# Attention feeding a soft mixture of experts: batch softmax steps moved ahead of V products, token maxima read from copied logits, exp(-m) added by TensorE

## The chip, the core and the metric

The kernel runs on one core of a Trainium2 chip. The core has a matrix engine (TensorE, PE in the profile; its weight loads are listed apart as PEld), a vector engine (VectorE, DVE), a scalar engine (ScalarE, ACT), a general engine (GpSimd, POOL) and SyncE (SP), which here only issues transfers. Every engine works through a queue of its own in order and waits on semaphores for the others. Matmuls write to PSUM, which this kernel uses as eight banks of 512 fp32 values per partition; everything else lies in SBUF. The metric is the time of one execution on the device in microseconds.

## The reference

Two parts follow each other. Attention over 8 batches, 12 heads, 448 positions and 64 columns has one unusual term, exp(-m), in the denominator; a soft mixture of experts then mixes all 3584 tokens into 32 slots and back.

```python
scores = scale * np.matmul(q, k.transpose(0, 1, 3, 2))
m = np.max(scores, axis=-1, keepdims=True)
e = np.exp(scores - m)
attn = e / (np.sum(e, axis=-1, keepdims=True) + np.exp(-m) + 1e-09)
x = attn @ v                                  # 3584 tokens x 768
logits = x @ phi                              # 3584 x 32
d = softmax of logits over the tokens         # each with + 1e-09 in its sum
slot_out = relu(d.T @ x @ w1) @ w2            # 32 slots, 4 for each of 8 experts
c = softmax of logits over the slots
return c @ slot_out                           # 3584 x 768
```

## The kernel before

**Pairs and slots.** The 96 heads are taken in 48 pairs n = 0 to 47 (NPAIR is 48), two heads in the two halves of the partitions; six pairs make a batch b. After a ramp written out by hand, the loop over s (line 758) runs one pair per turn in two half slots, y = 0 and 1. The order of the calls in that loop is the order of each engine's queue; a planner is not used. A half slot hs = 2s + y calls, in this order:

- `As` and `Bk`: score matmuls in one direction (`A`, lines 274 to 307) whose row maxima VectorE takes straight from PSUM (`mx`), and in the other direction (`Bk`, lines 352 to 404), with the maxima subtracted by a second matmul and the exponential taken by ScalarE (lines 372 and 402).
- in y = 1 the transposes of q and k of a later pair (`T`, line 256, copied out at line 263 by ScalarE or at 265 by VectorE), and for every third pair `W2` and `W3`, which turn the maxima and compute exp(-m) into the small tile `ec` (lines 345 and 348).
- `AV` (line 436): the exponentials times V. V has a 65th column of ones (D is 64), so the denominator falls out as one column of each of the seven blocks of `ps_av`. Of the 32 products of a pair, 12 come in y = 1, 12 in the next y = 0, and then 8 more for the last 64 positions.
- the functions in `post[hs]`, the batch softmax steps described below (line 788).
- in y = 1 `PX` (lines 494 to 507), which turns a finished pair of tokens into `xT`; in y = 0 the last 8 `AV` products and `N1` (line 449), a ScalarE copy of `ps_av` into `ubuf`; in y = 1 `N2` for that pair: VectorE adds 1e-9 and `ec` to the denominators (line 464) and takes the reciprocal (line 465), then GpSimd multiplies (lines 469, 479 and 480).
- transfers, copies of V and weight loads, all issued or done by GpSimd.

**Batch softmaxes.** `P(b)` returns six steps that run while the next pairs are in work, at half slots 2(6b + 8) + 0, 1, 2, 4, 5 and 9 for most batches. Step 0 multiplies x by phi (`l_mm`, 24 small matmuls, line 535), copies the logits from PSUM into `l`, a part of the tile `lb` (`l_ev`, ScalarE, line 558), and takes each token's maximum over the slots from PSUM (`c_max`, VectorE, line 562). Step 1 transposes the copied logits (`l_turn`, line 570), takes a column maximum (line 572) and subtracts the token maxima (`c_sub`, GpSimd, line 577). Step 2 spreads the column maximum (line 582), forms the running one (lines 583 and 585) and subtracts it (line 591). Step 3 takes exponentials (lines 596 and 601) and rescales the sums (line 607). Step 4 transposes one of the softmaxes (line 627, copied out at 628) and step 5 adds 28 small matmuls (line 623) to the sums (line 632).

**PSUM.** Score tiles `ps_a` and all PSUM tiles of the batch steps share one ring of three banks (`psA`); `ps_b`, `ps_t`, `ps_m` and `ps_x` share one of four (`psB`); `ps_av` has one bank. A new tile of a ring waits until the one three (or four) places earlier has been read.

Of the kernel before, what the change touches and what calls it, by code (L numbers as in the profile page):

```python
# [10 lines left out]
AX = mybir.AxisListType  # L11
AF = mybir.ActivationFunctionType
ALU = mybir.AluOpType
# [13 lines left out]
W65 = 65  # L27
# [4 lines left out]
def kernel(  # L32
# [10 lines left out]
    nc = tc.nc  # L43
    B, H, S, D = q.shape
# [112 lines left out]
    with ExitStack() as at:  # L157
# [182 lines left out]
        def W3(g):  # L340
            t = psm.tile([128, S], BF16, tag="mT", name="mT")
            nc.scalar.copy(t, st["ps_m"][:, 0:S])
            mT[g] = t
            e = psm.tile([128, NP, 7], F32, tag="ec", name="ec", bufs=3)
            nc.scalar.activation(e[:, :, 0:6].rearrange("p l (i h) -> p i l h", i=3),
                                 ngm[g][:, 0:18].rearrange("p (i l h) -> p i l h", i=3, h=2),
                                 AF.Exp, scale=scale)
            nc.scalar.activation(e[:, :, 6], ngm[g][:, 18:21], AF.Exp, scale=scale)
            ec[g] = e


# [69 lines left out]
        def AV(n, i, qs):  # L421
            g, pl = divmod(n, NP)
            if i == 0 and qs[0] == 0:
                av[n] = av_tile(n)
            a = av[n]
            if n == NPAIR - 1 and i == 0 and qs[0] == 3:
                av_half["ps"] = psA.tile([128, 512], F32, tag="a", name="ps_av")
            for u in qs:
                for hl in range(2):
                    if u < 3:  # L430
                        c0 = (2 * u + hl) * W65
                        o, qc = a[:, c0:c0 + W65], slice(u * 128, (u + 1) * 128)
                    else:
                        t, z = (av_half["ps"], 0) if n == NPAIR - 1 else (a, 6 * W65)
                        o, qc = t[64 - 64 * hl:128 - 64 * hl, z:z + W65], slice(384, 448)
                    nc.tensor.matmul(o, eT[n, i, hl][:, qc], vp[g % 2][:, 2 * pl + hl, i, 0:W65],  # L436
                                     start=(i == 0 and u == 0 and hl == 0) or (u == 3 and i == 0 and n == NPAIR - 1),
                                     stop=(i == 3), skip_group_check=True)

        av_half = {}  # L440
        on_pool = lambda n: n < NPAIR - 4
# [10 lines left out]
        def N2(n):  # L452
            g, pl = divmod(n, NP)
            b, pb = divmod(n, PB)
            u = us[n]
            eng = nc.gpsimd if on_pool(n) else nc.vector
            rec = psm.tile([128, 7], F32, tag="rec", name="rec", bufs=3)
            e = ec[mg(n)][:, group[n][1], :]
            if n == NPAIR - 1:
                nc.vector.scalar_tensor_tensor(rec[:, 6:7], av_half["ps"][:, D:W65], 1e-9, e[:, 6:7],  # L460
                                               op0=ALU.add, op1=ALU.add)
                nc.vector.scalar_tensor_tensor(rec[:, 0:6], u[:, 0:6, D], 1e-9, e[:, 0:6], op0=ALU.add, op1=ALU.add)
            else:
                nc.vector.scalar_tensor_tensor(rec, u[:, :, D], 1e-9, e, op0=ALU.add, op1=ALU.add)
            nc.vector.reciprocal(rec, rec)
            x = xb[b % 2]
            c = pb * 128
            rec2 = psm.tile([128, 2], F32, tag="rec2", name="rec2", bufs=3)
            eng.tensor_mul(  # L469
                x[:, 0:3, c:c + 128].rearrange("p i (h d) -> p i h d", h=2),  # L470
                u[:, 0:6, 0:D].rearrange("p (i h) d -> p i h d", h=2),
                rec[:, 0:6].rearrange("p (i h) -> p i h", h=2).unsqueeze(3).to_broadcast([128, 3, 2, D]))
            if n == NPAIR - 1:

                for h in range(2):
                    r = slice(64 - 64 * h, 128 - 64 * h)
                    nc.scalar.mul(x[r, 3, c + 64 * h:c + 64 * h + 64], av_half["ps"][r, 0:D], rec[r, 6:7])
                return
            eng.tensor_scalar(rec2, halfm, rec[:, 6:7], None, op0=ALU.mult)
            eng.tensor_mul(  # L480
                x[:, 3, c:c + 128].rearrange("p (h d) -> p h d", h=2),
                u[:, 6, 0:D].unsqueeze(1).to_broadcast([128, 2, D]),
                rec2.unsqueeze(2).to_broadcast([128, 2, D]))
# [32 lines left out]
        def P(b):  # L516
# [42 lines left out]

            def c_max():  # L560
                m = psm.tile([128, 4], F32, tag="cm", name="cm")
                nc.vector.reduce_max(m, v["ps_l"] if b < B - 1 else l[:, 0:4, :], axis=AX.X)
                v["cm"] = m

            def l_turn():
                if b == B - 1:
                    ps = v["ps_lT"]
                else:
                    ps = pa([128, 128], F32, "ps_lT")
                    nc.tensor.transpose(ps, flat(l[:, 0:4, :]), identf)  # L570
                m = psm.tile([128, 1], BF16, tag="sm", name="sm")
                nc.vector.reduce_max(m, ps, axis=AX.X)
                v["sm"] = m
                v["z"] = psm.tile([128, 9, NS], F32, tag="z", name="z", bufs=1)
# [75 lines left out]

            both = lambda *fs: (lambda: [f() for f in fs])
            if b < B - 1:
                return [both(lambda: l_mm(range(KC)), l_ev, c_max), both(l_turn, c_sub), both(s_max, d_sub),
                        both(exps, corr)] + ([c_turn, both(s_mm, s_add)] if late(b) else [both(s_mm, s_add), c_turn])
            return [lambda: l_mm([0]), lambda: l_mm([1]), lambda: l_mm([2]), lambda: l_mm([3]), lambda: l_mm([4]),
                    both(lambda: l_mm([PB - 1]), l_ev,
# [28 lines left out]
        def As(c):  # L685
            for _ in range(min(c, len(runs))):
                A(*runs.pop(0))
# [70 lines left out]
        for s in range(3, NPAIR + 1):  # L758
            for y in range(2):
                hs = 2 * s + y  # L760
                mix = len(runs) > 1 and runs[0][1] == 1 - y
                if mix:
                    Bk(s, 2 * y, mix=True)
                    Bk(s, 2 * y + 1, y, mix=True)
                else:
                    As(1)
                if mix:
                    pass
                elif s < NPAIR:
                    Bk(s, 2 * y)  # L770
                    side = int(y == 1 and len(runs) > 0 and runs[0][1] == 3)
                    Bk(s, 2 * y + 1, side)
                    As(1 - side)
                else:
                    As(1)
                if y == 0:
                    for i in (2, 3):
                        AV(s - 1, i, range(3))
                else:
                    if s < NPAIR - 6:  # L780
                        T(s + 6)
                    if s and s + 1 in firsts:
                        W2(mg(s + 1))
                        W3(mg(s + 1))
                    if s < NPAIR:
                        for i in (0, 1):
                            AV(s, i, range(3))
                for f in post.get(hs, ()):
                    f()
                if y and 0 <= s - 2 < NPAIR - 2:  # L790
                    PX(s - 2)
                if y == 0:
                    if 0 <= s - 1:
                        for i in range(4):
                            AV(s - 1, i, [3])
                        if s == NPAIR:
                            PX(s - 2)
                        N1(s - 1)
                        if not on_pool(s - 1):
                            N2(s - 1)  # L800
                else:
                    if 0 <= s - 1 and on_pool(s - 1):
                        N2(s - 1)
                if y == 0 and s and s + 1 in firsts:
                    W1(mg(s + 1))
                if y == 0 and wait_loads:
                    f, z = wait_loads.pop()
                    f(z)
                if y == 0 and s % 3 == 2 and (s + 1) // 3 < NG:
                    if s == NPAIR - 4:  # L810
                        V(NG - 1)
                    if s - 1 in half_at:
                        load_half(half_at[s - 1], 0, w_tile(half_at[s - 1]))
                if y == 0 and s - 1 in stage_at:
                    stage_rows(*stage_at[s - 1][0])
                if y == 0 and s - 2 in half_at:
                    load_half(half_at[s - 2], 1)
                if y == 0 and s - 2 in stage_at:
                    stage_rows(*stage_at[s - 2][1])
                if y == 0 and hs in rows_at:  # L820
                    load_rows(rows, rows_at[hs])
                    rows = rows_at[hs]
# [209 lines left out]
```

## Time and profile before

Three runs took 297.56, 299.5 and 299.66 us, with a median of 299.5. The profiled execution has a span of 299.0 us from its first to its last instruction.

| What | Value |
|---|---|
| span of the profiled execution | 299.0 us |
| GpSimd busy | 195.9 us, 66% of the span |
| granted TensorE clock | full up to about 254 us, 0.5 to 0.7 in the last stretch |
| main stretch of the batches | about 60 to 240 us, one batch of six pairs in 29.8 us |
| score maxima on VectorE (line 287) | 250 of 613 ns each |
| exponentials on ScalarE (line 372) | 250 of 574 ns each |
| exp(-m) on ScalarE (lines 345, 348) | 17 of 228 ns and 17 of 199 ns |

How to read it: each engine's busy time counts from an instruction's start to its end, so two neighbours that overlap in the pipeline count once. An entry of the waits names the instruction whose engine sat idle, and what ended the idle time. On TensorE the distance between the starts of two matmuls says more than their durations, which include the way through the array.

### The profile page before, as it was taken

Reading aid. Unit: us, or ns where it says so; the run is one execution under the profiler, and the core shown is the slowest. Engines: PE = TensorE matmul, PEld = TensorE weight load, DVE = VectorE, ACT = ScalarE, POOL = GpSimd, SP = SyncE. Lnnn points to the kernel's source line nnn. Section 1 sums busy time; section 2 is a strip of 40 time slices with the busy share of each in tenths; the row PEclk is TensorE's granted clock in tenths of the full one; section 3 lists DMA queues with packets and bytes.
Section 4 is the critical chain, followed back from the end, with each engine's and each line's share of the span. In section 5 each row is a group of like instructions: output and inputs, shape, how many; then the busy total and the mean of one; then the engine's idle time right before and its main releaser. Section 6 shows DMA issues by size and latency. Waiting matters only on the chain.

```text
span 299.0 us, 12398 instructions
## 1 busy us (share of the span) xinstructions
PE 271.4 (91%) x5174; PEld 162.5 (54%) x5174; DVE 249.7 (84%) x581; ACT 249.8 (84%) x559; POOL 195.9 (66%) x391
## 2 busy tenths in 40 slices
PE   5999899999999999999899999999999999996820
PEld 4445456566666566566556666656665555652100
DVE  5899799999999989999889999998999675537930
ACT  3569999999899989998989899989999987337820
POOL 8792887979696979887879697978686633000000
PEclk9999999999999999999999999999999999997555
DMA  7999998999999999999999999999799989908997
GB/s 132 147 143 208 149 138 138 188 165 188 185 204 179 184 176 202 163 182 182 202 159 184 176 199 152 196 183 196 125 150 187 213 185 263 344 10 318 380 453 322
DMA packets 47015, 58.67 MB, mean 196 GB/s; under 512 B 2800, under 2 KB 39920, under 8 KB 46704
## 3 DMA queue, kind: packets, MB, share of 16 engines
q0 software_dynamic: 40304, 42.29, 89.6%
q1 hardware_dynamic: 6656, 15.60, 13.8%
q8 instruction: 40, 0.66, 0.8%
q14 instruction: 15, 0.12, 0.1%
HBM read 89.16 MB, written 15.14 MB: 349 GB/s over the span
## 4 chain that ended last, share of the span: by engine, by line
PE 68%; ACT 10%; DVE 6%; POOL 6%; issue 4%; DMA 2%; DVEq 0%; POOLq 0%; ACTq 0%
PE ps_av L436 15%; PE ps_a L285 10%; PE ps_b L367 7%; PE ps_b L370 7%; PE ps_t L256 5%; PE ps_b L396 5%; PE ps_x L501 3%; PE ps_b L399 3%; ACT W L402 2%; PE ps_o L925 2%; DVE mx L298 2%; PE ps_s L623 2%; PE ps_h L862 2%; PE ps_so L882 2%; ACT W L263 2%
## 5 line engine op out<-in xcount | busy, mean ns | idle before, releaser
L287 DVE TENSOR_REDUCE mx<-ps_a 128x1 f32<-128x448 f32 x250 | 137.3, 613 | 4.6 <-PE ps_a L285 3.5
L372 ACT ACTIVATE W<-ps_b 128x448 bf16<-128x448 f32 x250 | 120.4, 574 | 0.0
L285 PE MATMUL ps_a<-W 64*128 64x448 bf16 x250 | 80.9, 352 | 0.0
L367 PE MATMUL ps_b<-W 64*128 64x448 bf16 x250 | 70.5, 352 | 1.1
L436 PE MATMUL ps_av<-W 128*128 128x65 bf16 (+1 forms) x1536 | 64.9, 196 | 2.2 <-issue 1.6
L436 PEld LDWEIGHTS <-W 128*128 128x128 bf16 (+1 forms) x1536 | 50.5, 100 | 30.2 <-issue 26.4
L370 PE MATMUL ps_b<-mT,sel 64*128 64x448 bf16 x250 | 66.5, 350 | 0.0
L469 POOL TENSOR_TENSOR W<-ubuf,rec 128x384 bf16<-128x384 f32 x44 | 36.3, 824 | 35.7 <-ACT W L507 19.3
L402 ACT ACTIVATE W<-ps_b 128x448 bf16<-128x448 f32 x86 | 46.1, 574 | 2.0 <-PE ps_b L399 2.0
L256 PEld LDWEIGHTS <-W 64*64 64x64 bf16 x1344 | 29.3, 112 | 12.7 <-issue 4.3
L507 ACT CAST W<-ps_x 128x512 bf16<-128x512 f32 x47 | 28.6, 608 | 7.4 <-PE ps_x L501 7.2
L256 PE MATMUL ps_t<-ident,W 64*64 64x64 bf16 x1330 | 30.6, 195 | 2.4 <-ACT W L215 1.4
L307 DVE TENSOR_REDUCE mx<-ps_a 128x1 f32<-128x448 f32 x48 | 29.5, 615 | 1.4 <-PE ps_a L304 1.4
L285 PEld LDWEIGHTS <-W 64*128 64x128 bf16 x250 | 23.4, 94 | 9.8
L114 POOL DMA_DIRECT2D W<-in_moe_w_dram x30 | 22.6, 755 | 7.9 <-PE ps_b L399 7.8
L370 PEld LDWEIGHTS <-sel 64*128 64x128 bf16 x250 | 19.6, 94 | 14.4 <-issue 5.6
L396 PE MATMUL ps_b<-W 64*64 64x448 bf16 (+1 forms) x134 | 27.1, 374 | 0.3
L449 ACT COPY ubuf<-ps_av 128x455 f32<-128x455 f32 x44 | 25.1, 571 | 0.8 <-POOL W L408 0.6
L399 PE MATMUL ps_b<-mT,sel 64*64 64x448 bf16 (+1 forms) x134 | 25.1, 354 | 0.1
L263 ACT COPY W<-ps_t 128x896 bf16<-128x896 bf16 x21 | 19.5, 927 | 6.5 <-PE ps_t L256 6.5
L298 DVE TENSOR_REDUCE mx<-ps_a 128x1 f32<-128x448 f32 x38 | 21.1, 616 | 1.9 <-PE ps_a L294 1.9
L480 POOL TENSOR_TENSOR W<-ubuf,rec 128x128 bf16<-128x128 f32 x44 | 17.5, 398 | 3.7
(156 smaller groups left out, 446.6 us busy)
## 6 DMA issues: line engine op xcount, KB each, us to landing
W<-in_moe_w_dram POOLq DMA_DIRECT2D x24, 768.0 KB, 9.9
W<-in_v_dram POOLq DMA_DIRECT2D x32, 192.0 KB, 6.5
out_dram<-W SPq DMA_DIRECT2D x2, 2688.0 KB, 10.0
W<-in_q_dram POOLq DMA_DIRECT2D x15, 336.0 KB, 6.3
W<-in_k_dram POOLq DMA_DIRECT2D x15, 336.0 KB, 7.5
stage<-in_moe_w_dram POOLq DMA_DIRECT2D x4, 768.0 KB, 9.6
W<-stage SPq DMA_DIRECT2D x4, 576.0 KB, 7.3
out_dram<-W SPq DMA_DIRECT2D x6, 384.0 KB, 3.0
```

Of the source, the lines that this page charges most:

```text
L256: nc.tensor.transpose(o, src[r, pl, tok * D:(tok + 1) * D], ident[r, r])
L285: nc.tensor.matmul(ps[:, 0:S], t[r, 0, i * 128:(i + 1) * 128], t[r, 1, :], start=True, stop=True)
L287: nc.vector.reduce_max(m[:, c:c + 1], ps[:, 0:S], axis=AX.X)
L307: nc.vector.reduce_max(mx[g][:, c:c + 1], ps[:, 0:S], axis=AX.X)
L367: nc.tensor.matmul(pss[hl][:, 0:S], t[rs[hl], 1, cols], t[rs[hl], 0, :], start=True, stop=False)
L370: nc.tensor.matmul(pss[hl][:, 0:S], sel[rs[hl], 2 * pl + hl:2 * pl + hl + 1].to_broadcast([64, 128]), mT[mg(n)][rs[hl], :], start=False, s ...
L372: nc.scalar.activation(e[:, hl, :], pss[hl][:, 0:S], AF.Exp, scale=scale)
L396: nc.tensor.matmul(outs[hl], t[rs[hl], 1, cols], t[rs[hl], 0, :], start=True, stop=False)
L399: nc.tensor.matmul(outs[hl], sel[rs[hl], 2 * pl + hl:2 * pl + hl + 1].to_broadcast([64, m]), mT[mg(n)][rs[hl], :], start=False, stop=True)
L402: nc.scalar.activation(e, p[:, 0:S], AF.Exp, scale=scale)
L436: nc.tensor.matmul(o, eT[n, i, hl][:, qc], vp[g % 2][:, 2 * pl + hl, i, 0:W65], start=(i == 0 and u == 0 and hl == 0) or (u == 3 and i == ...
L469: eng.tensor_mul(x[:, 0:3, c:c + 128].rearrange("p i (h d) -> p i h d", h=2), u[:, 0:6, 0:D].rearrange("p (i h) d -> p i h d", h=2), rec[: ...
```

## The change

Three edits. (1) Batch steps of half slots below 91 run right after the scores of their half slot, ahead of `T`, `W2`, `W3` and `AV`, where they ran after these. (2) For all batches but the last, the token maxima are taken from the copied logits, and one half slot later, in step 1. (3) The addition of exp(-m) to the denominators leaves VectorE. GpSimd adds 1e-9 to `ec`, once per group of pairs, and TensorE adds `ec` (fp32, seven columns) into the denominator columns of `ps_av` by a product with an fp32 identity, for pairs 0 to 46. VectorE then takes the reciprocal straight from `ubuf`. The last pair keeps two additions on VectorE.

```diff
@@ W3
             nc.scalar.activation(e[:, :, 6], ngm[g][:, 18:21], AF.Exp, scale=scale)
+            nc.gpsimd.tensor_scalar(e, e, 1e-9, None, op0=ALU.add)
             ec[g] = e
@@ AV
+            if i == 3 and qs[0] == 0 and n < NPAIR - 1:
+
+                nc.tensor.matmul(a[:, 0:7 * W65].rearrange("p (s c) -> p s c", c=W65)[:, :, D], identf,
+                                 ec[mg(n)][:, group[n][1], :], start=False, stop=True, skip_group_check=True)
@@ N2
             if n == NPAIR - 1:
-                nc.vector.scalar_tensor_tensor(rec[:, 6:7], av_half["ps"][:, D:W65], 1e-9, e[:, 6:7],
-                                               op0=ALU.add, op1=ALU.add)
-                nc.vector.scalar_tensor_tensor(rec[:, 0:6], u[:, 0:6, D], 1e-9, e[:, 0:6], op0=ALU.add, op1=ALU.add)
-            else:
-                nc.vector.scalar_tensor_tensor(rec, u[:, :, D], 1e-9, e, op0=ALU.add, op1=ALU.add)
-            nc.vector.reciprocal(rec, rec)
+                nc.vector.tensor_add(rec[:, 6:7], av_half["ps"][:, D:W65], e[:, 6:7])
+                nc.vector.tensor_add(rec[:, 0:6], u[:, 0:6, D], e[:, 0:6])
+            nc.vector.reciprocal(rec, rec if n == NPAIR - 1 else u[:, :, D])
@@ c_max
-                nc.vector.reduce_max(m, v["ps_l"] if b < B - 1 else l[:, 0:4, :], axis=AX.X)
+                nc.vector.reduce_max(m, l[:, 0:4, :], axis=AX.X)
@@ l_turn
                     nc.tensor.transpose(ps, flat(l[:, 0:4, :]), identf)
+                    c_max()
@@ P
-                return [both(lambda: l_mm(range(KC)), l_ev, c_max), both(l_turn, c_sub), both(s_max, d_sub),
+                return [both(lambda: l_mm(range(KC)), l_ev), both(l_turn, c_sub), both(s_max, d_sub),
@@ the loop over s
                     As(1)
+                early_post = hs < 2 * NPAIR - 5
+                if early_post:
+                    for f in post.get(hs, ()):
+                        f()
                 if y == 0:
                     for i in (2, 3):
                         AV(s - 1, i, range(3))
...
-                for f in post.get(hs, ()):
-                    f()
+                if not early_post:
+                    for f in post.get(hs, ()):
+                        f()
```

## The prediction

> **What bounds the kernel now.** I read the page first, then the chain of waits, then busy time by stretch, the list of waits, and last the timeline of single engines in one batch. The page's first part and the chain's shares by engine:
>
> ```profile
> PE 271.4 (91%) x5174; PEld 162.5 (54%) x5174; DVE 249.7 (84%) x581; ACT 249.8 (84%) x559; POOL 195.9 (66%) x391
> PE 68%; ACT 10%; DVE 6%; POOL 6%; issue 4%; DMA 2%; DVEq 0%; POOLq 0%; ACTq 0%
> ```
>
> TensorE holds most of the chain; VectorE and ScalarE little. By stretch (stretch in us, its length, then busy us and instruction counts of PE, PEld, DVE, ACT, POOL, the clock, the DMA share, GB/s), two batches:
>
> ```profile
> 61.20:91.00 29.80, 29.61 (x603) 18.82 (x602) 28.39 (x68) 28.85 (x68) 23.84 (x46) 1.00 1.15 185
> 91.00:120.80 29.80, 29.03 (x595) 18.30 (x593) 27.99 (x65) 28.26 (x67) 24.64 (x48) 1.00 1.14 184
> ```
>
> Three engines are 94 to 99% busy at full clock. Work taken from one of them alone frees at most the time in which the others waited for it, and work added to the one on the chain costs nearly all of itself. So the question is what VectorE's waits cost TensorE, against what TensorE is given. VectorE waits for the batch steps (engine, instruction, releaser: us, times, longest):
>
> ```profile
> DVE acc L632 <- PE ps_s L623: 3.0, 6, 1.5
> DVE cm L562 <- ACT lb L558: 2.6, 7, 0.5
> DVE sm L572 <- PE ps_lT L570: 2.5, 2, 1.4
> DVE lb L583 <- PE ps_bc L582: 1.8, 2, 1.4
> POOL W L469 <- ACT W L507: 19.3, 14, 1.9
> ```
>
> and in one batch its timeline shows how it falls behind (start, duration, instruction):
>
> ```profile
> 87.94 0.29 DVE L562 TENSOR_REDUCE cm<-ps_l 128x4 f32<-128x128 f32 x1 [0.45 <-ACT lb L558]
> 88.25 1.16 DVE L287 TENSOR_REDUCE mx<-ps_a 128x1 f32<-128x448 f32 x2
> ...
> 90.39 0.28 DVE L572 TENSOR_REDUCE sm<-ps_lT 128x1 bf16<-128x128 f32 x1
> 90.58 0.16 DVE L464 SCALAR_TENSOR_TENSOR rec<-ubuf,ec 128x7 f32<-128x7 f32 x1
> 90.78 0.20 DVE L465 RECIPROCAL rec<-rec 128x7 f32<-128x7 f32 x1
> 90.89 2.17 DVE L287 TENSOR_REDUCE mx<-ps_a 128x1 f32<-128x448 f32 x4
> ```
>
> TensorE in the same batch:
>
> ```profile
> 89.60 0.53 PE L436 MATMUL ps_av<-W 128*128 128x65 bf16 x12
> 89.97 0.30 PE L570 MATMUL ps_lT<-identf,lb 128*128 128x128 f32 x1
> 90.11 0.39 PE L501 MATMUL ps_x<-ident,W 128*128 128x128 bf16 x4
> ...
> 91.01 0.54 PE L367 MATMUL ps_b<-W 64*128 64x448 bf16 x2
> 91.20 0.53 PE L370 MATMUL ps_b<-mT,sel 64*128 64x448 bf16 x2
> 91.52 0.35 PE L285 MATMUL ps_a<-W 64*128 64x448 bf16 x1
> ```
>
> A couple of score matmuls starts 0.19 us after the last one (91.01 to 91.20), but the score tile at 91.52 comes 0.32 after its neighbour: 0.13 us lost because the ring of three banks still waits for VectorE's maxima. The same shows at 93.11 (0.13), 100.80 (0.12) and 111.21 (0.23), each behind a batch step: 0.6 us per batch, 7 x 0.6 = 4.2 us over the run. That is what VectorE's lateness at the batch steps costs; it is far less than its idle time.
>
> **The fp32 product.** 47 times TensorE gets a 128x128 fp32 weight load and seven moving columns, in the middle of the V products. The built program has 5268 matmuls and as many loads, 94 more than before, so each product is two of both. No trace shows this operation. Bound below: two pairs of load and matmul at the V products' rate, 12 in 0.37 us (89.60 to 89.97), 31 ns each: 0.06 us. Bound above: the only fp32 matmul in the trace, line 570, holds its place for 0.14 us (89.97 to 90.11), with 128 columns instead of 7; twice, 0.28 us. It can't be a gain, since nothing leaves TensorE for it. Between them: the rows of line 570 give its weight load 142 ns (1.0 us over 7), those of line 436 97 ns, so an fp32 load is 45 ns longer; part of that lies under the neighbour, as the bf16 load does wholly. I take 31 + 30 = 60 ns for each of the two, 0.12 us in all, nearer to the V pair since seven columns hardly stream: 47 x 0.12 = +5.6 us, with ends 2.8 and 13.3. TensorE has the chain there, so I count all of it.
>
> The Trainium skill (page "TensorE: Matmul & The Clock Gate", section "Weight-path perf modes — Fast Weight Load (FWL) and DoubleRow") says that the fast weight load is off for FP32; the 142 against 97 ns agrees.
>
> **VectorE's side of it.** The addition of line 464 goes: from 90.58 to 90.78, 0.20 us of its queue, 47 x 0.20 = 9.4 us of VectorE, 1.2 per batch. The reciprocal reads seven spaced columns as the addition did and stays at 0.20. Off the chain this is worth nothing by itself; its worth is in the 4.2 us.
>
> **Token maxima.** The wait for ScalarE's copy (0.45 us at 87.94, 2.6 in all) goes, as the copy is then half a slot old, and the logits' bank is freed by the copy alone. The 0.29 us of reduction stay, behind the seven maxima of the next half slot. The subtraction on GpSimd that needs it (line 577, 0.41 us at 89.25) then waits until about 89.2 to 89.6, and behind it stands line 469, which in this batch waits until 91.12 anyway: nothing.
>
> **Steps moved ahead.** They issue no transfers. The order of ScalarE's queue doesn't change, and on VectorE only the step's result now stands ahead of the copy of line 265, whose tile is used six pairs later. In y = 0 all 20 V products end when they did, and so does the copy after them. In y = 1 the transposes and V products come 0.06 (line 627) to 0.7 us (line 623, 28 matmuls, 109.00 to 109.71) later, the transfer into xT when it did. VectorE gets its input 0.4 to 0.9 us earlier. The cover that goes: the step's bank must be free at once. Line 570 would issue at 88.86, and the tile three places back is reduced by about 88.8, earlier still without the 0.45 us; line 627 at 98.27 against about 98.1 (five maxima from 95.42 at 0.535 us), with its input from ScalarE at 97.99; line 623 at 108.09 against 108.03. It holds, with little to spare; where it does not, a step costs up to one maximum, 0.5 us.
>
> Edits 1 to 3 together take VectorE's waits (about 1 us per batch) and 1.2 us of its work. Of the 4.2 us I count four fifths, -3.4 us, since one or two steps may stall on their bank.
>
> **GpSimd.** 17 additions to a 128x21 tile; the nearest row is line 314 on 128x21, 280 ns: 4.8 us, one per three pairs. It waits for ScalarE's line 348, and the pair's multiplications (469) are queued behind. At 89.66 GpSimd would wait until 90.55 and end at 90.83, before the 91.12 at which line 469 starts: hidden. At 105.04 it would delay line 469 by 0.45 us, and GpSimd idles 1.88 us at 108.94. Its idle time of 19.3 us before line 469 covers it: 0, up to +1 if a late V copy follows (TensorE waited 0.6 us for line 314 at 104.06). The first product of each group waits for this addition, a slot after it: nothing. The last pair's two additions cost what the old ones did.
>
> **Sum.** +5.6 - 3.4 = +2.2 us. The profiled span of 299.0 us lies 0.5 under the median of 299.5; the sum is added to the median: 301.7 us.
>
> **Rivals.** (a) The fp32 product is dear: each of its two passes holds TensorE as long as line 570 does, 13.3 - 3.4 = +9.9 us, 309; half way, 0.20 us each, +6, 305.5. For it: the only fp32 row. Against: it has 18 times the columns. It makes the kernel slower by over 1% from 0.14 us per product on ((3.0 + 3.4) / 47), close to my 0.12, so 0.28 for it. The Trainium skill (page "FP8 and Floating Point Precision", section "TensorE Precision Notes") says that true FP32 takes four passes; no trace here shows one, and four of 60 ns would give 11.3 - 3.4, 307.4 us. (b) TensorE was held by VectorE more than the 4.2 us tell: with 2.2 us per batch less to do and to wait for, VectorE also gets ahead of the scores, and the product costs its lower bound. 2.8 us against 4.2 and as much again of the other waits of TensorE (at 95.61 and 99.56 a couple of line 367 comes 0.15 to 0.2 us late): 299.5 + 2.8 - 7 = 295.3. For it: three engines as close as this wait for each other in turn. Against: VectorE has 6% of the chain. 0.18. (c) The moved steps stall on their banks, three per batch by 0.25 us, and the 4.2 us stay: 299.5 + 5.6 + 5 = 310 at worst, 305 if they only cancel the gain; the margins of 0.06 to 0.2 us above speak for it, VectorE's earlier place against it. 0.12. (d) The first reading, +2.2: 0.42.
>
> **How the numbers follow.** One per cent, about what a measurement of this kernel can tell from no change, is 296.5 to 302.5. The forecast's own range is 299 to 304, of which some three quarters lie within: same 0.32 and slower 0.10. (a) gives slower 0.25 and same 0.03, (b) faster 0.17 and same 0.01, (c) slower 0.08 and same 0.04. Sums: faster 0.17, same 0.40, slower 0.43. The range reaches from (b) to most of (a): 295 to 308.
>
> **What would show it.** Line 442 of the new trace: two loads and two matmuls per pair, and the next V product 0.15 us (0.12 + 0.03) after the last one before them; 0.3 would mean (a). The 0.13 us ahead of score tiles behind the batch steps gone, or still there (c). The waits of lines 562, 572, 583 and 632 gone from VectorE's list, and VectorE less busy by about 8 us. TensorE's busy share in a batch at 99%. If ScalarE or VectorE had set the pace and TensorE's share falls, the sum is wrong in kind.

## The result, and the profile after

The changed kernel took 310.46 us (median of 4 runs, 310.06 to 311.56) against 298.84 us before: ratio 1.0393, 95% interval [1.0355, 1.0432], 11.6 us slower. The forecast was 301.7 us with a range of 295 to 308, so both were wrong. Four of the kernels below had one execution that was slower than their others (303 to 760 us); medians and ratios leave it out. The profiled execution of the changed kernel has a span of 309.7 us. The page's first part and the chain's shares by engine:

```profile
PE 281.4 (91%) x5268; PEld 172.3 (56%) x5268; DVE 247.1 (80%) x534; ACT 252.7 (82%) x559; POOL 201.5 (65%) x408
PE 70%; ACT 15%; DVE 7%; issue 3%; DMA 1%; DVEq 0%; ACTq 0%
```

TensorE has 10 us more busy time, and VectorE 2.6 less, where the prediction had 8. ScalarE's copies of the V sums lie 30.8 to 30.9 us apart for six pairs in most batches. In the trace of before they lie 28.9 to 29.6 us apart, and 30.8 to 31.3 only around 148.9 us, where TensorE stands still for 1.1 us and the profile shows nothing that it waits for; the 29.8 us given for a batch before is too long. Busy time of two such batches (columns as in the prediction):

```profile
61.20:92.03 30.83, 30.35 (x608) 19.46 (x605) 27.43 (x58) 28.40 (x65) 24.48 (x48) 1.00 1.14 180
92.03:122.86 30.83, 30.36 (x607) 19.45 (x606) 27.55 (x59) 28.51 (x66) 25.23 (x49) 1.00 1.10 175
```

The batch is 1.2 to 1.9 us longer. VectorE and ScalarE are now idle for 2.3 to 3.4 us of such a stretch (1.0 to 1.8 before), and only TensorE stays at 98%. From the list of waits:

```profile
DVE mx L287 <- PE ps_a L285: 18.0, 34, 2.0
POOL z L580 <- DVE cm L564: 9.3, 6, 1.7
POOL ec L349 <- ACT ec L348: 9.0, 10, 1.2
```

VectorE now idles 18.0 us for score tiles (3.5 before): it is early, and TensorE is late. The other two rows are GpSimd's waits that the change adds. VectorE's timeline at the first steps of a batch, and the V products of TensorE:

```profile
90.45 1.16 DVE L287 TENSOR_REDUCE mx<-ps_a 128x1 f32<-128x448 f32 x2 [0.97 <-PE ps_a L285]
91.52 0.62 DVE L307 TENSOR_REDUCE mx<-ps_a 128x1 f32<-128x448 f32 x1
92.06 0.28 DVE L564 TENSOR_REDUCE cm<-lb 128x4 f32<-128x128 f32 x1
92.25 0.29 DVE L575 TENSOR_REDUCE sm<-ps_lT 128x1 bf16<-128x128 f32 x1
92.44 0.62 DVE L265 COPY W<-ps_t 128x896 bf16<-128x896 bf16 x1
92.98 0.20 DVE L467 RECIPROCAL rec<-ubuf 128x7 f32<-128x7 f32 x1
```

```profile
94.53 0.52 PE L437 MATMUL ps_av<-W 128*128 128x65 bf16 x12
94.89 0.36 PE L442 MATMUL ps_av<-ec,identf 128*128 128x7 f32 x2
95.19 0.32 PE L437 MATMUL ps_av<-W 128*64 128x65 bf16 x8
```

The token maximum (92.06) waits for nothing and the addition ahead of the reciprocal is gone, as the change says. Part of what the prediction hoped for came, too. In both kernels most score tiles that follow a matmul of line 370 (371 now) start within 20 ns of it. From the first to the seventh copy of the logits, the gaps of over 25 ns there add up to 4.7 us in the trace of before and to 2.6 us here. But from the start of the fp32 product (94.89) to the next V product 0.30 us pass. The groups of the product, by form (busy us, mean ns of one):

```profile
L442 PE MATMUL ps_av<-ec,identf 128*128 128x7 f32 x94 | 17.0, 253 | 0.0
L442 PEld LDWEIGHTS ps_av<-ec,identf 128*128 128x128 f32 x94 | 14.2, 191 | 0.0
```

By the starts of single matmuls in this trace, the first pass comes 34 ns after the last V product on 128 columns, the second 107 ns after the first, and the first V product on 64 columns 185 ns after that: 326 ns in all. In the trace of before the same step, 128 to 64 columns with nothing between, takes 125 ns. So a product holds TensorE for 0.20 us.

### The profile page after: what moved, and what is told of

Read it like the earlier page. It is cut to its first block, busy times and chain, and to the rows that moved or that the text cites. A ratio compares the mean times of both kernels' runs of the same rounds, so it can differ in the third digit from the quotient of the medians.

```text
span 309.7 us, 12520 instructions
## 1 busy us (share of the span) xinstructions
PE 281.4 (91%) x5268; PEld 172.3 (56%) x5268; DVE 247.1 (80%) x534; ACT 252.7 (82%) x559; POOL 201.5 (65%) x408
## 4 chain that ended last, share of the span: by engine, by line
PE 70%; ACT 15%; DVE 7%; issue 3%; DMA 1%; DVEq 0%; ACTq 0%
PE ps_av L437 14%; PE ps_a L285 9%; PE ps_b L368 7%; PE ps_b L371 6%; PE ps_t L256 5%; PE ps_b L397 5%; ACT W L403 4%; ACT W L263 4%; DVE mx L287 3%; PE ps_av L442 3%; ACT W L509 3%; PE ps_b L400 3%; PE ps_x L503 2%; PE ps_o L933 2%; DVE mx L298 2%
## 5 line engine op out<-in xcount | busy, mean ns | idle before, releaser
L287 DVE TENSOR_REDUCE mx<-ps_a 128x1 f32<-128x448 f32 x250 | 140.6, 619 | 21.8 <-PE ps_a L285 18.0
L437 PE MATMUL ps_av<-W 128*128 128x65 bf16 (+1 forms) x1536 | 66.8, 196 | 0.6 <-ACT ubuf L454 0.5
L256 PEld LDWEIGHTS <-W 64*64 64x64 bf16 x1344 | 27.7, 112 | 9.8 <-issue 2.8
L307 DVE TENSOR_REDUCE mx<-ps_a 128x1 f32<-128x448 f32 x48 | 29.6, 616 | 0.6 <-PE ps_a L304 0.6
L454 ACT COPY ubuf<-ps_av 128x455 f32<-128x455 f32 x44 | 24.3, 553 | 4.1 <-POOL ngm L314 2.8
L298 DVE TENSOR_REDUCE mx<-ps_a 128x1 f32<-128x448 f32 x38 | 21.2, 619 | 2.1 <-PE ps_a L294 1.9
L503 PE MATMUL ps_x<-ident,W 128*128 128x128 bf16 x192 | 18.7, 219 | 1.5 <-ACT W L263 1.3
```

The lines of the kernel that those rows point to most:

```text
L256: nc.tensor.transpose(o, src[r, pl, tok * D:(tok + 1) * D], ident[r, r])
L287: nc.vector.reduce_max(m[:, c:c + 1], ps[:, 0:S], axis=AX.X)
```

## The experiments

Every kernel was measured beside the kernel before on the same chip; a gain or loss is given against that.

**Each edit alone.** Edit 3 (fp32 product) is the diff of W3, AV and N2 above; edit 1 is the diff of the loop; edit 2 the diff of c_max, l_turn and P.

> The kernel before with edit 3 alone (exp(-m) added by TensorE as an fp32 product, the VectorE addition gone). Theory 1, the fp32 product holds TensorE: in the changed kernel a V product on 128 columns is followed by the first on 64 columns 0.125 us later without, and 0.326 us later (34 + 107 + 185 ns) with the product between them, so 0.20 us per pair, 9.4 us over 47 pairs; 306 to 309 us. Theory 2, the product is cheap and the moved steps cost the time: within 1% of before.

306.12 against 298.36 us, ratio 1.0258 [1.0234, 1.0283]: +7.8 us, as theory 1 has it.

> The kernel before with edit 1 alone (batch steps ahead of T, W2, W3 and AV). Theory 1: moving gains up to 4 us of score tiles that wait for VectorE, and costs about as much, because in y = 1 a step on all 128 rows now stands between the 64-row tiles of Bk and T: 298 to 302 us. Theory 2, the moved steps stall on their banks and hold up everything: 305 us or more.

302.46 against 298.36 us, 1.0137 [1.0113, 1.0162]: +4.1 us, just above the range of the first theory, short of the second.

> The kernel before with edit 2 alone (token maxima from the copied logits, half a slot later). Theories 1 and 2: VectorE loses 2.6 us of waits, TensorE at most 1 us of its 4.2; 298 to 300 us. If GpSimd's wait for the maxima (9.3 us in the changed kernel) held the chain, 302 us or more.

300.61 against 298.36 us, 1.0080 [1.0054, 1.0107]: +2.3 us. Neither theory had this: an edit that takes 2.6 us of waits from VectorE costs time.

> Edits 1 and 2 together, exp(-m) added on VectorE as before. If the three edits add up, 298.4 + 4.1 + 2.3 = 304.8 us; the changed kernel less what the fp32 product cost alone gives 310.5 - 7.8 = 302.7 us, so 302.5 to 305.

302.03 against 298.72 us, 1.0123 [1.0095, 1.0152]: +3.3 us by the medians and 3.7 by the ratio. No cost of edit 2 on top of edit 1 can be told, and 7.8 + 3.3 to 3.7 = 11.1 to 11.5 us is nearly the whole loss.

The traces tell the same by parts. A batch is taken here from one copy of the logits to the next, the shortest of the second to the fifth; the gaps are those ahead of score tiles as above; the end runs from the last copy of the logits to the end of the span. One trace each:

| Kernel | against before, us | batch, us | gaps, us | end, us |
|---|---|---|---|---|
| before, with a third buffer for the score maxima (see below) | no difference | 28.97 | 4.6 | 44.2 |
| edit 1 | +4.1 | 29.64 | 3.2 | 44.2 |
| edit 1, steps of y = 1 alone | +2.4 | 29.43 | 3.6 | 44.1 |
| edit 1, steps of y = 0 alone | +1.4 | 29.19 | 3.7 | 44.4 |
| edit 2 | +2.3 | 29.39 | 7.1 | 44.8 |
| edits 1 and 2 | +3.3 | 29.64 | 2.5 | 44.2 |
| edit 3 | +7.8 | 29.91 | 2.8 | 45.0 |
| fp32 product in addition | +8.8 | 30.20 | 4.4 | 45.0 |
| edit 3 with a bf16 product | +1.2 | 28.88 | 2.8 | 46.5 |
| all three edits | +11.6 | 30.80 | 2.6 | 45.0 |

**The price of the fp32 product.** First the product in addition to everything that was there:

```diff
+                nc.tensor.matmul(a[:, 7 * W65:7 * W65 + 7], identf, ec[mg(n)][:, group[n][1], :],
+                                 start=False, stop=True, skip_group_check=True)
```

> The kernel before, with the fp32 product issued in addition, into seven unused columns of the V bank that nothing reads; VectorE and GpSimd do what they did. Measures the price of the product alone. Theory 1: +7 to +9.4 us, 306 to 309 us. Theory 2: within 1% of before.

307.19 against 298.36 us, 1.0296 [1.0276, 1.0316]: +8.8 us, of the 9.4 that 47 times 0.20 us make. The batch is 1.23 us longer, which is six times 0.20; 0.8 of the 8.8 us lie in the longer end. Against edit 3 alone (+7.8) it shows what the rest of that edit, no addition on VectorE and one more on GpSimd, gives back: about 1.0 us, where 9.4 us of VectorE's queue went.

Then the same sum without the fp32 passes:

```diff
-            e = psm.tile([128, NP, 7], F32, tag="ec", name="ec", bufs=3)
+            e = psm.tile([128, NP, 7], BF16, tag="ec", name="ec", bufs=3)
...
-                nc.tensor.matmul(a[:, 0:7 * W65]..., identf,
+                nc.tensor.matmul(a[:, 0:7 * W65]..., ident,
```

> Edit 3 with a bf16 product: exp(-m) is written in bf16 and added by TensorE with the bf16 identity; the 1e-9 is left out for pairs 0 to 46, and GpSimd gets nothing. Theory 1 (the fp32 passes are what costs): one V-like product, 0.03 us per pair, +1.5 us, less what VectorE's 0.20 us per pair gives; 297.5 to 300 us. Rival (the place of the product or the lost overlap on VectorE costs): 304 us or more.

299.58 against 298.34 us, 1.0031 [1.0009, 1.0053]: +1.2 us. Here the product adds 9 ns by the starts where a 64-column tile follows (34 + 100 instead of 125) and 26 to 27 ns elsewhere, about 0.7 us. So of edit 3's 7.8 us some 6.6 are the fp32 passes, together with GpSimd's 17 additions, which this kernel leaves out as well. The 1.2 us that stay are not in the batches, which are 0.09 us shorter than without any product (28.88 against 28.97); the end of the run is longer (46.5 us, of it 0.7 in a stall of TensorE, against 44.2), and why no run shows.

**The moved steps.** Edit 1 split by half slot (`early_post = y == 1 and hs < 2 * NPAIR - 5`, and the same with y == 0), and once with the steps of y = 1 one place further down:

```diff
                     if s and s + 1 in firsts:
                         W2(mg(s + 1))
                         W3(mg(s + 1))
+                    if early_post:
+                        for f in post.get(hs, ()):
+                            f()
                     if s < NPAIR:
                         for i in (0, 1):
                             AV(s, i, range(3))
```

> Edit 1 for the steps of y = 1 alone (1, 4 and 5), ahead of T as in the change; the steps of y = 0 stay. Theory 1 (a 128-row step between the 64-row tiles of Bk and T costs two changes of the tile shape: 0.21, 0.20 and 0.18 us more per step by the starts in the trace of edit 1 alone, 0.6 us per batch): 301.5 to 302.5 us against 298.4 before. Theory 2 (the moved steps wait for their bank): most of edit 1's 4.1 us is in step 2, where the start of line 582 comes 0.53 instead of 0.28 us after its neighbour, and this kernel is within 1 us of before.

300.79 against 298.34 us, 1.0071 [1.0042, 1.0101]: +2.4 us, between the two theories, nearer to the first.

> The steps of y = 1 moved to stand behind T, W2 and W3 and ahead of AV, where the tile shape changes anyway. Theory 1: no extra change of shape, VectorE still gets its input 0.4 us earlier; 297.5 to 299.5 us. Theory 2: as the kernel with these steps ahead of T.

298.19 against 298.34 us, 0.9984 [0.9961, 1.0008]: no difference.

> Edit 1 for the steps of y = 0 alone (0, 2 and 3). The rest of edit 1's 4.1 us, after 2.4 for the steps of y = 1: theory 1, the matmul of line 582 now asks for its bank 0.4 us earlier than VectorE frees it and waits 0.25 us, six or seven times, 1.5 to 1.8 us; 299.5 to 300.5 us. If the two halves of edit 1 only hurt together: 298 to 299 us.

300.13 against 298.72 us, 1.0050 [1.0032, 1.0068]: +1.4 us, as theory 1 has it.

TensorE's timeline with edit 1 alone:

```profile
89.64 0.35 PE L399 MATMUL ps_b<-mT,sel 64*64 64x448 bf16 x2
89.92 0.33 PE L570 MATMUL ps_lT<-identf,lb 128*128 128x128 f32 x1
90.19 0.63 PE L256 MATMUL ps_t<-ident,W 64*64 64x64 bf16 x28
...
92.71 0.35 PE L285 MATMUL ps_a<-W 64*128 64x448 bf16 x1
93.25 0.22 PE L582 MATMUL ps_bc<-ident,sm 128*128 128x128 bf16 x1 [0.19 <-DVE mx L287]
```

and with the steps of y = 1 behind T and W2:

```profile
88.69 0.35 PE L399 MATMUL ps_b<-mT,sel 64*64 64x448 bf16 x2
88.88 0.60 PE L256 MATMUL ps_t<-ident,W 64*64 64x64 bf16 x28
...
89.59 0.19 PE L337 MATMUL ps_m<-ident,W 128*128 128x64 bf16 x1
89.62 0.31 PE L570 MATMUL ps_lT<-identf,lb 128*128 128x128 f32 x1
89.77 0.53 PE L436 MATMUL ps_av<-W 128*128 128x65 bf16 x12
```

The fourth field is the shape in the array. In the second kernel the transposes follow the last 64x64 scores after 0.19 us, and line 570, among 128x128 work, takes 0.15 us more. In the first a single 128x128 matmul stands between two runs of 64x64 tiles: 0.28 us to it and 0.27 from it, 0.55 in place of 0.19 + 0.15. Summed over the three steps of y = 1 that is 0.6 us per batch, six batches, 3.6 us; the gaps ahead of score tiles give back 1.0 us of it (4.6 to 3.6), near the 2.4 measured. The list of waits also names VectorE's maxima as releaser of line 570's weight load, six times for 2.1 us in all, but that isn't what costs: line 623, for which it names no releaser, starts after the same 0.28 us. The same steps, moved past V products only, cost nothing and gain nothing. In y = 0 the wait is the bank's: line 582 starts 0.54 us after its neighbour, where line 535 at the same place mostly takes 0.28 to 0.30, and VectorE's maximum ended the wait. That is the margin that the prediction found for steps 1, 4 and 5 and didn't work out for step 2.

**The token maxima.** Half of the edit, the source without the place (only the diff of c_max):

> Half of edit 2: the token maxima are taken from the copied logits, but in step 0 where they were. Theory 1 (in its old place the maximum stood in a hole, since the next score maximum waits there for GpSimd; moved by half a slot it is 0.3 us more of VectorE at a full place): 298 to 299 us, as before. Rival: reading SBUF or the wait for the copy is what costs, and this is as slow as edit 2 alone, 300.6 us.

298.47 against 298.34 us, 1.0000 [0.9982, 1.0018]. So the place costs. With edit 2 alone the profile names a new wait:

```profile
DVE mx L287 <- POOL W L314: 4.5, 6, 0.8
```

A third buffer (`tag="mx", name="mx", bufs=3`) takes it away, with edit 2 and without:

> Edit 2 alone, with a third buffer for the tile of score maxima, so that VectorE no longer waits for GpSimd's negation at the place where the token maximum stood. Theory 1 (the hole): that wait of 0.77 us per batch goes and the kernel comes back to before or under it, 297.5 to 299 us. Rival (GpSimd, held by its wait for the late maxima, is what costs): as edit 2 alone, 300.6 us.

300.56 against 298.72 us, 1.0066 [1.0043, 1.0088]: still +1.8 us. My expectation failed.

> Control: the kernel before with the third buffer for the score maxima alone. The token maximum in its old place still waits for ScalarE's copy, which ends later than GpSimd's negation here, so 298 to 299 us, as before; if the wait for GpSimd costs elsewhere too, up to 1.5 us less.

298.26 against 298.72 us, 0.9985 [0.9968, 1.0003]: as before.

The two timelines show why. Edit 2 with the third buffer:

```profile
88.39 1.16 DVE L287 TENSOR_REDUCE mx<-ps_a 128x1 f32<-128x448 f32 x2 [0.63 <-PE ps_a L285]
...
90.52 0.28 DVE L562 TENSOR_REDUCE cm<-lb 128x4 f32<-128x128 f32 x1
...
90.91 0.39 DVE L464 SCALAR_TENSOR_TENSOR rec<-ubuf,ec 128x7 f32<-128x7 f32 x1
...
91.46 2.16 DVE L287 TENSOR_REDUCE mx<-ps_a 128x1 f32<-128x448 f32 x4
...
92.08 0.35 PE L285 MATMUL ps_a<-W 64*128 64x448 bf16 x1
```

and the third buffer alone:

```profile
88.14 0.29 DVE L562 TENSOR_REDUCE cm<-ps_l 128x4 f32<-128x128 f32 x1 [0.46 <-ACT lb L558]
...
88.38 1.16 DVE L287 TENSOR_REDUCE mx<-ps_a 128x1 f32<-128x448 f32 x2
...
90.72 0.16 DVE L464 SCALAR_TENSOR_TENSOR rec<-ubuf,ec 128x7 f32<-128x7 f32 x1
...
91.03 2.22 DVE L287 TENSOR_REDUCE mx<-ps_a 128x1 f32<-128x448 f32 x4
...
91.70 0.35 PE L285 MATMUL ps_a<-W 64*128 64x448 bf16 x1
```

The score maximum starts at 88.38 or 88.39 in both. The hole was there, but with GpSimd's wait removed another one ends at the same time, the score tile itself, which TensorE delivers after the 24 logit matmuls. In that hole the token maximum and its wait for ScalarE cost nothing. Half a slot later VectorE has no hole; the maximum, and a longer addition behind it (0.39 us, with no reason shown, against 0.16), make the next score maxima 0.43 us later (91.46 against 91.03), and the score tile that waits for their bank 0.38 us later (92.08 against 91.70). Six times 0.38 is 2.3 us; edit 2 costs 2.3 us alone and 1.8 with the third buffer. Why edit 2 costs nothing beside edit 1 was not tried; the batches there are equally long (29.64 us each), and with edit 1 TensorE is later at this place, which would give the hole back.

**What is left.** The parts that cost nothing, without and with the bf16 product:

> The kernel before with the steps of y = 1 between W3 and AV and the third buffer for the score maxima. Each alone was 0.15% under before with an interval that holds 1. If the two gains are real and add, 297.4 to 298.0 us; if they were noise, as before.

298.26 against 298.91 us, 0.9979 [0.9956, 1.0002]: not told from before.

> The same with the bf16 product for exp(-m) in place of VectorE's addition (1e-9 left out for pairs 0 to 46). Theory 1, TensorE holds the pace: the product costs 0.03 us or more per pair also here, 298.5 to 300 us. Rival, VectorE's relief only needed the steps in the right place to count: under 297.5 us, faster than both kernels.

299.83 against 298.91 us, 1.0030 [1.0001, 1.0059], and 1.6 us over the kernel beside it. Here too the loss is not in the batches: the last copy of the logits starts at 251.1 us, 0.7 earlier than in the kernel beside it (251.8). But from there to the end it takes 45.9 us in place of 44.2, although TensorE's last product comes at the same distance within 0.2 us; the two largest transfers of the output take 12.0 us in place of 10.3. So in these two traces VectorE's relief gains a little, and the end of the run takes more than that away; why the transfers take longer is open. No version found is faster than the kernel before.

## Why the prediction was wrong

- **What bounds the kernel: right.** TensorE has the chain and 98% of a batch, and what it is given costs nearly all of itself: 8.8 of 9.4 us.
- **The fp32 product: right in kind, mis-sized.** I took 0.12 us, "nearer to the V pair since seven columns hardly stream"; it holds TensorE 0.20 us by the starts, and costs 8.8 us instead of 5.6: 3.2 of the 9.4 us by which the sum was off. Few columns did not make it cheap: the second pass comes 107 ns after the first, and the weight load lasts 191 ns, longer than the 142 of the row I had. With another number of columns it was not tried. Rival (a) had its half-way value, 0.20 us, in its text, at a chance of 0.28. The Trainium skill (page "FP8 and Floating Point Precision", section "TensorE Precision Notes") has four passes for true FP32; the trace shows two loads and two matmuls per product, and what happens inside each it doesn't show.
- **The 3.4 us given back: the step that failed most, wrong in sign, 6.2 of the 9.4 us.** The relief came in part: the gaps ahead of score tiles fell from 4.7 to 2.6 us, 2.1 where I had counted 3.4, and edit 3's share of the relief is worth about 1.0 us of time. But the moves themselves, which I had priced at nothing, cost TensorE more: edits 1 and 2 lose 3.3 to 3.7 us. With 8.8 - 1.0 + 3.3 to 3.7 = 11.1 to 11.5 of 11.6 us the sum nearly closes.
- **"It holds, with little to spare": right on the banks in y = 1, and blind to the tile shape.** For the steps of y = 1 no bank wait of size showed. What I priced at nothing was the tile shape: I let each step issue where the transposes had started, and counted only its own length. It costs 0.6 us per batch, and the trace of before has it already, 0.28 us from the 64x64 scores to the V products where the transposes follow after 0.19. In y = 0 line 582 did wait for its bank, 0.25 us a time. Rival (c) named stalls on banks and missed the larger part.
- **The wait for ScalarE's copy "goes, as the copy is then half a slot old": it went, and nothing was gained.** Here the wait stood in a hole of the queue and was free, and the moved maximum costs 2.3 us with edit 2 alone. I listed the wait as a cost because the waits put a releaser beside it, and did not ask when the next instruction could have started without it.
- **GpSimd: as said.** Its additions take 273 ns each (280 taken), its new waits of 9.3 and 9.0 us are long, and no run shows that they cost.
- The profiled execution of before was a late one: in the runs here the time lies some 1.8 us over the span (297.8 us with 296.0), so its span of 299.0 belongs to about 300.8 us; the stall of 1.1 us at 148.9 is part of it. The sum was added to the median and isn't moved by that.

## What to carry to other kernels

Before moving work off an engine that waits, ask when its next instruction could start if the wait were gone: if another input arrives at the same time, the wait is worth nothing, and the same work at a fuller place costs its whole length. Check as well that the new place adds nothing on the engine that holds the chain. There, price an operation by the spacing of starts around it, with its neighbours' tile shapes, not by how little data it streams. Keep small matmuls next to work of the same tile shape.

## What the runs showed that I had not expected

- An fp32 product of 128x128 by seven columns spaces its two passes by 107 ns, as much as three and a half V products of 65 bf16 columns (29 to 31 ns each); the same product in bf16 takes 34 + 100 ns in place of 125, so 9 ns.
- A change of tile shape has a price of its own: 64x64 scores to 64x64 transposes 0.19 us, to a 128x128 matmul 0.28 us, and from line 570 back to the transposes 0.27 us where line 570 ahead of 128x128 work takes 0.14 to 0.15.
- With exp(-m) added by TensorE the end of the run is longer, though TensorE has the same to do there: 45.0 us with the fp32 product and 45.9 to 46.5 with the bf16 one, against 44.2. No run shows why.
